# Value products of an attention kernel as two tiles of 64 features, with a new order in its slots

## The chip, the cores and the metric

The kernel runs on one core of a Trainium2 chip. The metric is the device time of one execution, in microseconds (us). Below, PE is the tensor engine's matmuls, PEld its weight loads, DVE the vector engine, ACT the scalar engine, POOL the GpSimd engine, and SP the engine whose queue issues the DMAs; SPq is that queue.

## The reference, cut to what matters

```python
def phi(x):
    proj = np.einsum('bhsd,df->bhsf', x, w_phi)                    # d = 64, f = 128
    proj = proj - np.max(np.abs(proj), axis=-1, keepdims=True)
    return np.concatenate([np.exp(proj), np.exp(-proj)], axis=-1)  # 256 features
q_p, k_p = phi(q), phi(k)                    # batch 4, heads 8, sequence 576
kv = np.einsum('bhsf,bhsd->bhfd', k_p, v)
z = np.sum(k_p, axis=2)
num = np.einsum('bhsf,bhfd->bhsd', q_p, kv)
den = np.einsum('bhsf,bhf->bhs', q_p, z)[..., None] + 1e-06
x = num / den                                # then [2304, 512]
h = (x @ w1) * (x @ w2) @ w3 @ w_out         # first MLP
y = np.maximum(h @ w_in, 0.0) ** 2 @ w_out2  # second MLP
```

The MLP weights arrive as 64-bit floats and are decoded on the chip.

## The kernel before, in words

Attention is worked off in 16 units t = 0 to 15, one for each pair of heads of a batch (`todo`). The sequence of 576 is cut in 512 and a tail of 64; the tails of two units are handled together, in the even unit. A list of words, `SLOT` (L32 to L38), is the order of the work in a slot: for each t the loop at L668 calls the step of every word in turn, and a step adds its instructions at the end of the queue of each engine that it uses. A word works on unit t plus an offset (`steps`, L594): `project_q`, `max_q`, `minus_q`, `values0` on unit t; `turn_k`, `turn_q` on t+1; `out`, `feature_sums`, `denominators`, `reciprocals`, `quotients` on t-1; `store_x` on t-2; the loads on t+2. Words that begin with w (`w0`, `w1`, `w-1`) advance the decoding of one weight tile by a step: a DMA of raw words, an ACT copy, twice two DVE operations (L107/L110 and L114/L117), a POOL addition, an ACT copy, a POOL subtraction. `START` (L28) holds words that run ahead of the first slot. Each engine works its queue strictly in this order.

A slot begins on PE with `project_q` (L371): for both heads and for the tail, three passes each (high by high, high by low, low by high parts), into the tile pq (three PSUM banks, one buffer: the next unit's `project_q` can't write until the `exp_q` steps of this unit have read it). Then `project_k` (pk, L243), `turn_k` and `turn_q` (transposes, L279), `max_rows` (pm, L386), `out` (po, L446, two matmuls of 64 output features side by side), `feature_sums` (pd: L461 with four tiles of 32, then L467 with two tiles of 64), `minus_q` (L405), `values` (pkv, L420 and for the tail L429).

The maximum of a row of q takes a way round: `max_q` on DVE (L378), a transpose on PE (L386), `max_parts` on DVE (L391 to L394), two DMAs from mh into the row tile mrow (L397), and `minus_q`, which adds it to pq with a matmul. Then ACT exponentiates pq twice, `exp_q0` and `exp_q1` (L412). For k, `peak_k` (DVE, L339) and `less_k` (DVE, L349) lead to `exp_k` (ACT, L356), which makes kp, the stationary operand of `values`; part 2 of k (the tails) exists in even slots only.

`values` loads 128 features by 128 positions of kp for each matmul and streams 65 columns of v and ones:

```python
for s in range(2):
    for c in range(C):
        nc.tensor.matmul(
            z["pkv"][:, s, j], z["kp", j][:, c, s, :], z["vs"][:, j, c, :],
            start=j + s + c == 0, stop=False, skip_group_check=True,
        )
```

These are fp32 matmuls, and the profile shows each as two records of weight load and matmul: 32 for a unit's 16 matmuls of `values` and 4 for its tail.

In the last slots the words that occur once (`once`, L639) add the beginning of the first MLP: x is loaded back (`x_load`), split in high and low parts (`x_split0` to `x_split3`), and multiplied (`product_a0`, `product_a1`, `product_b`). From `prefetch` (L553) raw weight words for the MLPs are loaded on the same SP queue as `store_x` (L518), which stores the finished x of two units. The MLPs follow from about 232 us on and are not touched, apart from the place of one store.

Of the kernel before, what the change touches and what calls it, by code (L numbers as in the profile page):

```python
# [9 lines left out]
F32 = mybir.dt.float32  # L10
# [16 lines left out]

START = """  # L28
turn_q/-1 turn_k/-1 high_q/-1 high_k/-1 turn_tails/-1 low_q/-1 low_k/-1 keep_tails/-1 low_tail/-1
""".split()  # L30
SLOT = """
load_kq product_b project_q keep_values project_k0 turn_w3b split_w3b x_load max_q project_k1 w1 w1 w0 turn_k peak_k0  # L32
max_rows x_split0 high_k max_parts w-1 store_x less_k0 out x_split2 exp_k0 feature_sums x_split1 peak_k1 less_k1
keep turn_q low_k turn_tails project_k2 exp_k1 denominators spread high_q peak_k2 less_k2 minus_q keep_tails
values0 gate turn_w3 x_split3 low_q w0 exp_q0 exp_k2 w0 exp_q1 w0 product_a0 values1 keep_rest low_tail reciprocals
split_w3 product_a1 quotients keep_a load_v tail_values
""".split()


# [1 line left out]
def attention_then_mlps(ctx: ExitStack, tc: tile.TileContext, q, k, v, w_phi, w1, w2, w3, wo, wi2, wo2, out):  # L41
# [155 lines left out]
    with ExitStack() as actx:  # L197
# [55 lines left out]
        def load_kq(t):  # L253
            (b, pr), z = todo[t], live[t]
            z["nm"], z["b"], z["pr"] = f"{b}_{pr}", b, pr
            z["before"] = live[t - 1] if t else None
            z["qm"] = load_q(b, pr)
            z["km"] = load_k(b, pr)
            if pr == 0:
                tails[b] = load_tail(q, b, "qtl"), load_tail(k, b, "ktl")  # L260
            z["qt"], z["kt"] = tails[b]
# [98 lines left out]
        def project_q(z):  # L360

            pr = z["pr"]
            z["pq"] = ps.tile([P, 3 * 512], F32, tag="q", bufs=1, name=f"pq_{z['nm']}")
            z["pv"] = z["pq"][:, 0:2 * S]
            tT = (z if pr % 2 == 0 else z["before"])["tT"]
            r = pr % 2
            sides = [(j, j * C * P, z["qT"], C * P) for j in range(2)] + [(r, 2 * C * P, tT, P)]
            for n, (a, b) in enumerate(((0, 0), (0, 1), (1, 0))):
                for j, at, src, width in sides:
                    h = slice(j * D, (j + 1) * D)  # L370
                    nc.tensor.matmul(  # L371
                        z["pq"][:, at:at + width], wss[h, b, :], src[h, a, 0:width], start=n == 0, stop=n == 2
                    )

        def max_q(z):

# [32 lines left out]
        def exp_q(z, s):  # L409
            if s == 0:  # L410
                z["qp"] = att.tile([P, 2, 2 * S], F32, tag="qp", name=f"qp_{z['nm']}")
            nc.scalar.activation(z["qp"][:, s], z["pv"], AF.Exp, scale=1.0 - 2.0 * s)  # L412

        def values(z, j):

            if j == 0:
                z["pkv"] = bank(f"pkv_{z['nm']}")[:, 0:4 * (D + 1)].rearrange("p (s j d) -> p s j d", s=2, j=2)
            for s in range(2):
                for c in range(C):
                    nc.tensor.matmul(  # L420
                        z["pkv"][:, s, j], z["kp", j][:, c, s, :], z["vs"][:, j, c, :],
                        start=j + s + c == 0, stop=False, skip_group_check=True,
                    )

        def tail_values(z):
            pr = z["pr"]
            kpt = z["kp", 2] if pr % 2 == 0 else z["before"]["kp", 2]
            for s in range(2):
                nc.tensor.matmul(  # L429
                    z["pkv"][:, s].rearrange("p j d -> p (j d)"), kpt[:, pr % 2, s, :],  # L430
                    z["vt"][:, pr].rearrange("p j d -> p (j d)"), start=False, stop=True, skip_group_check=True,
                )

        def keep_values(z):

# [15 lines left out]
        def feature_sums(z):  # L451

            z["pd"] = pd = bank(f"pd_{z['nm']}", "o", 2)
            for e in range(2):
                for i in range(4):
                    j, s = divmod(i, 2)
                    for k, (at, of, n) in enumerate(
                        ((0, j * C * P, HALF),) if s == 0 else
                        ((0, j * C * P + HALF, C * P - HALF), (C * P - HALF, 2 * C * P + j * TAIL, TAIL))
                    ):  # L460
                        nc.tensor.matmul(  # L461
                            pd[i * 32:(i + 1) * 32, at:at + n], z["zs"][:, e, j, :], z["qp"][:, e, of:of + n],
                            start=e + k == 0, stop=e == 1, skip_group_check=True,
                        )
            for e in range(2):
                for j in range(2):
                    nc.tensor.matmul(  # L467
                        pd[j * D:(j + 1) * D, HALF:HALF + TAIL], z["kv"][:, e, j, :],
                        z["qp"][:, e, 2 * C * P + j * TAIL:2 * C * P + (j + 1) * TAIL],
                        start=False, stop=e == 1, skip_group_check=True,  # L470
                    )

        def keep(z):
            z["nd"] = att.tile([P, S], F32, tag="nd", name=f"nd_{z['nm']}")
# [4 lines left out]

        def denominators(z):  # L480

            dc = att.tile([P, nb // 2], F32, tag="dc", name=f"dc_{z['nm']}")
            nc.vector.tensor_reduce(
                dc, z["pd"][:, 0:HALF].rearrange("p (n r) -> p n r", r=32), AX.X, ALU.max, apply_transpose=True
            )
# [76 lines left out]
        beside = [decode_splitting(rows(wo, j), f"wo{j}", wos) for j in range(NG)]  # L562
        beside += [decode_splitting(*w12_of(i), w12) for i in range(6)]
        beside += [decoding(*w3_of(i), w3s) for i in range(4)]
        load_kq(0)
# [5 lines left out]
        wst = att.tile([D, F], F32, bufs=1, name="wst")  # L571
        nc.sync.dma_start(wst, w_phi)
# [91 lines left out]
        with tc.manual_schedule(engines=mine):  # L664
# [226 lines left out]
    with tc.manual_schedule(engines=mine):  # L891
# [5 lines left out]
        for s, (grp, at, k) in enumerate(steps):  # L897
# [157 lines left out]
```

## Time and profile before

| what | us |
|---|---|
| median of 3 runs (lowest, highest) | 993.65 (989.38, 996.88) |
| the profiled execution's own time | 995.93 |
| its span from first to last instruction | 994.2 |
| PE busy in the span | 969.9 |
| DVE, ACT, POOL busy | 550.3, 377.8, 239.5 |

The profile is of one execution. Its span is divided by the start of `project_q` into a start of 9.2 us, the slots 0 to 15 up to about 225 us, a transition, and the MLPs. A row of a timeline gives start, length, engine, line, operation, tiles and, in brackets, how long the engine was idle before and what ended that. A row of windows gives the stretch and its length, then the busy time (and count) of PE, PEld, DVE, ACT and POOL, the granted clock of PE as a share of full speed, the share of the DMA engines in use and the GB/s.

### The profile page before, as it was taken

What the parts mean: (1) busy time and instruction counts of PE and PEld (TensorE: products, weight loads), DVE (VectorE), ACT (ScalarE), POOL (GpSimd) and SP (SyncE); (2) the same over time, 40 slices, a digit from 0 to 9 for tenths busy, and PEclk for the clock granted to TensorE, in tenths of its full rate; (3) what the DMA queues carried; (4) which work ended last, traced back from release to release, by engine and by line L of the source; (5) the groups of instructions that cost most, each with busy time, mean ns of one, the idle gap of its engine ahead of it and who ended that gap; (6) DMA issues with size and microseconds to landing.
All of it is one profiled execution on the core that took longest, in us unless ns stands there. A gap on an engine that the chain in (4) does not pass through costs nothing.

```text
span 994.2 us, 13665 instructions
## 1 busy us (share of the span) xinstructions
PE 969.9 (98%) x5304; PEld 796.1 (80%) x5304; DVE 550.3 (55%) x908; ACT 377.8 (38%) x689; POOL 239.5 (24%) x304
## 2 busy tenths in 40 slices
PE   6999999998999999999999999999999999999997
PEld 5788787776888898888888888888888888888896
DVE  5668888776665546566675487873223222322332
ACT  3556666663332233343333243442223212322322
POOL 2345555524222112333332135540000000000000
PEclk8879999999899999999999999999999999999999
DMA  5344545533323223424444432312000100100010
GB/s 146 95 117 133 144 134 144 159 108 104 108 86 127 64 106 127 149 102 152 149 170 154 164 106 91 100 43 84 1 1 32 55 1 0 64 1 1 1 43 22
DMA packets 81105, 89.16 MB, mean 90 GB/s; under 512 B 44624, under 2 KB 65680, under 8 KB 81040
## 3 DMA queue, kind: packets, MB, share of 16 engines
q1 hardware_dynamic: 81040, 88.28, 27.9%
q8 instruction: 42, 0.69, 0.3%
q14 instruction: 23, 0.19, 0.1%
HBM read 69.76 MB, written 18.35 MB: 89 GB/s over the span
## 4 chain that ended last, share of the span: by engine, by line
PE 93%; DMA 3%; DVE 2%; issue 1%; ACT 0%; SPq 0%; DVEq 0%; ACTq 0%
PE op L875 20%; PE ph L176 20%; PE yp L857 10%; PE pb L176 9%; PE pa L176 9%; PE pkv L420 6%; PE pf L814 4%; PE pk L243 3%; PE po L446 2%; PE pq L371 2%; DMA mrow<-mh 1%; PE pd L461 1%; PE pq L405 1%; PE pkv L429 1%; PE pw L170 1%; PE pkt L279 1%
## 5 line engine op out<-in xcount | busy, mean ns | idle before, releaser
L875 PE MATMUL op<-w_w,r 128*128 128x512 f32 x864 | 214.5, 396 | 0.0
L875 PEld LDWEIGHTS op<-w_w,r 128*128 128x128 f32 x864 | 161.5, 188 | 37.4 <-ACT r L1005 0.5
L176 PE MATMUL ph<-y,w_w 128*128 128x512 f32 (+1 forms) x768 | 166.6, 366 | 0.0
L999 DVE SCALAR_TENSOR_TENSOR r<-ph,t 128x512 f32<-128x512 f32 (+1 forms) x80 | 51.1, 638 | 196.0 <-ACT t L997 196.0
L176 PEld LDWEIGHTS ph<-y,w_w 128*128 128x128 f32 x768 | 133.6, 189 | 26.5
L997 ACT ACTIVATE t<-ph 128x512 f32<-128x512 f32 (+1 forms) x80 | 44.4, 555 | 224.2 <-PE ph L176 224.2
L857 PE MATMUL yp<-g,w3o 128*128 128x512 f32 (+1 forms) x480 | 109.4, 378 | 0.0
L857 PEld LDWEIGHTS yp<-g,w3o 128*128 128x128 f32 x480 | 85.4, 192 | 16.4
L176 PE MATMUL pa<-c,w_w12a 128*128 128x512 f32 (+1 forms) x432 | 95.7, 369 | 0.8 <-ACT c L141 0.8
L176 PE MATMUL pb<-c,w_w12b 128*128 128x512 f32 (+1 forms) x432 | 93.9, 367 | 0.0
L122 POOL TENSOR_TENSOR dt_w<-dt_w,dy_w 128x512 f32<-128x512 f32 x48 | 62.7, 1306 | 123.5 <-DVE dy_w L117 122.4
L176 PEld LDWEIGHTS pa<-c,w_w12a 128*128 128x128 f32 x432 | 75.0, 189 | 16.4 <-ACT c L141 1.1
L176 PEld LDWEIGHTS pb<-c,w_w12b 128*128 128x128 f32 x432 | 75.2, 189 | 13.4
L1007 DVE TENSOR_TENSOR r<-r,r 128x512 fp32r<-128x512 f32 (+1 forms) x80 | 51.0, 638 | 41.2 <-ACT r L1005 37.0
L936 DVE TENSOR_TENSOR g<-pb,a 128x512 f32<-128x512 f32 (+1 forms) x39 | 24.8, 636 | 86.6 <-PE pb L176 86.4
L132 POOL TENSOR_TENSOR w_w<-dt_w,w_w 128x512 fp32r<-128x512 f32 x32 | 48.8, 1525 | 89.8 <-ACT w_w L130 89.8
L1005 ACT ACTIVATE r<-r 128x512 fp32r<-128x512 f32 (+1 forms) x80 | 47.2, 590 | 55.5 <-DVE r L999 55.5
L420 PE MATMUL pkv<-vs,kp 128*128 128x65 f32 x512 | 65.0, 289 | 0.0
L420 PEld LDWEIGHTS pkv<-vs,kp 128*128 128x128 f32 x512 | 63.6, 206 | 0.8
L496 POOL COPY rc<-rc 32x9 f32<-32x9 f32 x128 | 35.7, 279 | 90.4 <-DVE rc L488 85.9
L938 ACT ACTIVATE g<-g 128x512 fp32r<-128x512 f32 (+1 forms) x39 | 23.0, 589 | 90.7 <-DVE g L936 90.7
L356 ACT ACTIVATE kp<-kp 128x512 f32<-128x512 f32 (+1 forms) x80 | 46.9, 587 | 17.4 <-DVE kp L349 16.1
(134 smaller groups left out, 1312.2 us busy)
## 6 DMA issues: line engine op xcount, KB each, us to landing
x<-x_hbm SPq DMA_DIRECT2D x16, 512.0 KB
raw_w<-in_moe_w_dram SPq DMA_DIRECT2D x16, 512.0 KB
raw_w<-in_moe_w_in_dram SPq DMA_DIRECT2D x16, 512.0 KB
raw_w<-in_moe_w_out_dram SPq DMA_DIRECT2D x16, 512.0 KB
qm<-in_q_dram SPq DMA_DIRECT2D x32, 128.0 KB
km<-in_k_dram SPq DMA_DIRECT2D x16, 256.0 KB
vs<-in_v_dram SPq DMA_DIRECT2D x32, 128.0 KB
raw_wo<-in_moe_w_out_dram SPq DMA_DIRECT2D x8, 512.0 KB
```

Source lines behind the costliest of these rows:

```text
L122: nc.gpsimd.tensor_tensor(out=w, in0=t.bitcast(F32), in1=e.bitcast(F32), op=ALU.add)
L132: nc.gpsimd.tensor_tensor(out=dst[:, 1], in0=w[0], in1=dst[:, 0].bitcast(F32), op=ALU.subtract)
L176: nc.tensor.matmul(ps[:, 0:n], a, c, start=kk + i == 0, stop=kk == KD - 1 and i == 2)
L356: nc.scalar.activation(z["kp", j][:, :, s, :], z["kp", j][:, :, 1, :], AF.Exp, scale=1.0 - 2.0 * s)
L420: nc.tensor.matmul(z["pkv"][:, s, j], z["kp", j][:, c, s, :], z["vs"][:, j, c, :], start=j + s + c == 0, stop=False, skip_group_check=True,)
L814: nc.tensor.matmul(pf, a, c, start=g + j + n == 0, stop=g == 1 and j == 3 and n == 2)
L857: nc.tensor.matmul(blk.yp[i][:, 0:blk.n], a, d, start=c % HG + s == 0, stop=c % HG == HG - 1 and s == 2)
L875: nc.tensor.matmul(ops[i], a, d, start=j + s == 0, stop=j == NR - 1 and s == 2)
L997: nc.scalar.activation(t[:, 0:n], ph[:, 0:n], AF.Relu)
L999: nc.vector.scalar_tensor_tensor(out=r32[:, 0:n], in0=ph[:, 0:n], scalar=0.0, in1=t[:, 0:n], op0=ALU.max, op1=ALU.mult)
L1005: nc.scalar.activation(r[:, 0, 0:n], r32[:, 0:n], AF.Copy)
L1007: nc.vector.tensor_tensor(out=r[:, 1, 0:n], in0=r32[:, 0:n], in1=r[:, 0, 0:n].bitcast(F32), op=ALU.subtract)
```

## The change

`values` and `tail_values` issue each matmul as two, one for each half of the features, which go to two column tiles of the PE array beside each other. `project_q` does all three passes of the heads before those of the tail. `feature_sums` puts L467 ahead of L461. The addition of 1e-6 moves from DVE to POOL, into the eight copies of `spread`, and the reciprocal moves behind these, into `reciprocals`. The load of w_phi is issued behind the loads of the first q. `SLOT` gets another order: `less_k0` ahead of `max_parts`; `exp_k0` ahead of `out`; `high_q`, then `exp_k2`, ahead of `keep_tails` and `exp_q0` on ACT; the splits of x behind `exp_k0`; `product_a0` ahead of `minus_q`. The first slot gets its own order through `START`. The last `store_x` is issued after the second step of the first MLP.

```diff
 START = """
 turn_q/-1 turn_k/-1 high_q/-1 high_k/-1 turn_tails/-1 low_q/-1 low_k/-1 keep_tails/-1 low_tail/-1
+project_q/0 project_k0/0 project_k1/0 max_q/0 peak_k0/0 less_k0/0 exp_k0/0 max_rows/0 max_parts/0 load_kq/0 w-1/0
+turn_q/0 turn_k/0 high_q/0 peak_k1/0 less_k1/0 low_q/0 project_k2/0 exp_k1/0 high_k/0 low_k/0 peak_k2/0 less_k2/0 values0/0 exp_k2/0
 """.split()
 SLOT = """
 load_kq product_b project_q keep_values project_k0 turn_w3b split_w3b x_load max_q project_k1 w1 w1 w0 turn_k peak_k0
-max_rows x_split0 high_k max_parts w-1 store_x less_k0 out x_split2 exp_k0 feature_sums x_split1 peak_k1 less_k1
-keep turn_q low_k turn_tails project_k2 exp_k1 denominators spread high_q peak_k2 less_k2 minus_q keep_tails
-values0 gate turn_w3 x_split3 low_q w0 exp_q0 exp_k2 w0 exp_q1 w0 product_a0 values1 keep_rest low_tail reciprocals
-split_w3 product_a1 quotients keep_a load_v tail_values
+max_rows high_k less_k0 max_parts w-1 store_x exp_k0 out x_split0 x_split1 x_split2 feature_sums peak_k1 less_k1
+keep turn_q low_k turn_tails project_k2 product_a0 exp_k1 denominators spread peak_k2 less_k2 high_q minus_q exp_k2
+keep_tails exp_q0 values0 gate turn_w3 x_split3 low_q w0 w0 exp_q1 w0 values1 keep_rest low_tail reciprocals split_w3
+product_a1 quotients keep_a load_v tail_values
 """.split()
...
             z["qm"] = load_q(b, pr)
+            if t == 0:
+                nc.sync.dma_start(wst, w_phi)
             z["km"] = load_k(b, pr)
...
-            sides = [(j, j * C * P, z["qT"], C * P) for j in range(2)] + [(r, 2 * C * P, tT, P)]
-            for n, (a, b) in enumerate(((0, 0), (0, 1), (1, 0))):
-                for j, at, src, width in sides:
-                    h = slice(j * D, (j + 1) * D)
-                    nc.tensor.matmul(
+            for sides in ([(j, j * C * P, z["qT"], C * P) for j in range(2)], [(r, 2 * C * P, tT, P)]):
+                for n, (a, b) in enumerate(((0, 0), (0, 1), (1, 0))):
+                    for j, at, src, width in sides:
+                        h = slice(j * D, (j + 1) * D)
+                        nc.tensor.matmul(
...
+        halves_f = [slice(0, F // 2), slice(F // 2, F)]
+
         def values(z, j):
...
             for s in range(2):
                 for c in range(C):
-                    nc.tensor.matmul(
-                        z["pkv"][:, s, j], z["kp", j][:, c, s, :], z["vs"][:, j, c, :],
-                        start=j + s + c == 0, stop=False, skip_group_check=True,
-                    )
+                    for h in halves_f:
+                        nc.tensor.matmul(
+                            z["pkv"][h, s, j], z["kp", j][:, c, s, h], z["vs"][:, j, c, :],
+                            start=j + s + c == 0, stop=False, skip_group_check=True,
+                        )
...
-            dc = att.tile([P, nb // 2], F32, tag="dc", name=f"dc_{z['nm']}")
+            z["dc"] = att.tile([P, nb // 2], F32, tag="dc", name=f"dc_{z['nm']}")
...
-            nc.vector.tensor_scalar(out=dc, in0=dc, scalar1=1e-6, scalar2=None, op0=ALU.add)
-            z["rc"] = att.tile([P, nb // 2], F32, tag="rc", name=f"rc_{z['nm']}")
-            nc.vector.reciprocal(z["rc"], dc)
...
-                    nc.gpsimd.tensor_copy(
-                        z["rc2"][i * 32:(i + 1) * 32, s, :], z["rc"][at * 32:(at + 1) * 32, :]
+                    nc.gpsimd.tensor_scalar(
+                        out=z["rc2"][i * 32:(i + 1) * 32, s, :], in0=z["dc"][at * 32:(at + 1) * 32, :],
+                        scalar1=1e-6, scalar2=None, op0=ALU.add,
                     )
 
         def reciprocals(z):
+            nc.vector.reciprocal(z["rc2"], z["rc2"])
...
-                    if f"{name}/{t}" not in START:
+                    if f"{name}/{t}" not in START and not (name == "store_x" and t > len(todo)):
                         step(name, t)
...
                 fold.product()
+            if s == 1:
+                store_x(live[-1])
```

`tail_values` is cut in two as `values` is, and in `feature_sums` the loop of L467 stands ahead of that of L461 with the start flags moved.

## Rows read from the trace of the kernel before

**Rows 1.** The page, busy time of the engines over the span.
```profile
PE 969.9 (98%) x5304; PEld 796.1 (80%) x5304; DVE 550.3 (55%) x908; ACT 377.8 (38%) x689; POOL 239.5 (24%) x304
```

**Rows 2.** Windows, one a slot: slots 0 to 3, 8, 9, and 15.
```profile
9.20:27.50 18.30, 15.85 (x73) 14.34 (x73) 9.53 (x18) 6.69 (x11) 1.27 (x1) 0.76 0.55 146
27.50:41.75 14.25, 14.25 (x112) 11.63 (x111) 9.87 (x19) 8.03 (x15) 4.44 (x10) 0.83 0.34 93
41.75:57.70 15.95, 14.78 (x113) 12.13 (x112) 10.34 (x21) 8.57 (x16) 8.26 (x15) 0.85 0.41 105
57.70:72.40 14.70, 14.70 (x114) 11.98 (x113) 9.95 (x19) 8.03 (x15) 4.61 (x10) 0.82 0.45 132
...
121.50:133.80 12.30, 12.30 (x114) 9.88 (x114) 10.38 (x21) 8.58 (x16) 6.13 (x13) 1.00 0.41 110
133.80:146.00 12.20, 12.20 (x114) 9.83 (x113) 9.84 (x19) 8.12 (x15) 6.67 (x13) 1.00 0.53 152
...
208.70:233.00 24.30, 22.02 (x178) 16.39 (x177) 12.54 (x24) 11.82 (x22) 6.42 (x14) 1.00 0.33 110
```

**Rows 3.** Timeline of PE in slot 8 and the first row of slot 9.
```profile
127.87 0.45 PE L467 MATMUL pd<-qp,kv 128*64 128x64 f32 x8
128.25 0.66 PE L279 MATMUL pqt<-ident,qm 128*128 128x128 f32 x4
128.67 0.60 PE L243 MATMUL pk<-wbd,tT 128*128 128x256 f32 x3
129.10 0.69 PE L405 MATMUL pq<-mrow,minus 128*128 128x512 f32 x3
129.63 3.73 PE L420 MATMUL pkv<-vs,kp 128*128 128x65 f32 x32
133.20 0.67 PE L429 MATMUL pkv<-vt,kp 128*128 128x130 f32 x4
133.79 0.73 PE L371 MATMUL pq<-qT,wss 64*128 64x512 f32 x3
```

**Rows 4.** Timeline of ACT in slots 8 and 9.
```profile
129.83 1.13 ACT L412 ACTIVATE qp<-pq 128x1152 f32<-128x1152 f32 x1
130.86 0.86 ACT L356 ACTIVATE kp<-kp 128x256 f32<-128x256 f32 x2
131.62 1.11 ACT L412 ACTIVATE qp<-pq 128x1152 f32<-128x1152 f32 x1
...
142.17 2.15 ACT L412 ACTIVATE qp<-pq 128x1152 f32<-128x1152 f32 x2
```

**Rows 5.** Timeline of DVE in slots 8 and 9.
```profile
125.59 0.67 DVE L349 TENSOR_TENSOR kp<-pk,kmax 128x512 f32<-128x512 f32 x1
...
129.30 0.42 DVE L339 TENSOR_REDUCE kmax<-pk 128x2 f32<-128x256 f32 x1
129.76 0.42 DVE L349 TENSOR_TENSOR kp<-pk,kmax 128x256 f32<-128x256 f32 x1
...
135.08 1.38 DVE L378 TRANSPOSE_TENSOR_REDUCE m<-pq 128x36 f32<-128x1152 f32 x1 [1.36 <-PE pq L371]
```

**Rows 6.** The chain that ended last, in order of time: three waits for a DMA.
```profile
48.59 1.91 DMA mrow<-mh
...
213.80 3.32 DMA mrow<-mh
...
242.12 4.87 DMA raw_w12b<-in_moe_w_dram
```

**Rows 7.** Waits of the SP queue, 215 to 256 us: total, times, longest.
```profile
SPq L521 <- POOL xm L511: 16.5, 1, 16.5
```

**Rows 8.** Windows of two stretches in which the granted clock was half.
```profile
18.70:32.35 13.65, 13.65 (x61) 12.70 (x62) 5.39 (x9) 6.16 (x12) 2.54 (x2) 0.50 0.34 93
...
52.83:63.07 10.24, 10.24 (x48) 9.48 (x47) 3.17 (x4) 3.21 (x8) 4.04 (x4) 0.50 0.36 90
```

**Rows 9.** Timeline of PE in slot 0, its value products.
```profile
19.52 7.03 PE L420 MATMUL pkv<-vs,kp 128*128 128x65 f32 x32
```

More of the change, by code (lines that the diff above doesn't have):

```diff
@@ L366, in project_q @@
             r = pr % 2
-            sides = [(j, j * C * P, z["qT"], C * P) for j in range(2)] + [(r, 2 * C * P, tT, P)]
-            for n, (a, b) in enumerate(((0, 0), (0, 1), (1, 0))):
-                for j, at, src, width in sides:
-                    h = slice(j * D, (j + 1) * D)
-                    nc.tensor.matmul(
-                        z["pq"][:, at:at + width], wss[h, b, :], src[h, a, 0:width], start=n == 0, stop=n == 2
-                    )
+            for sides in ([(j, j * C * P, z["qT"], C * P) for j in range(2)], [(r, 2 * C * P, tT, P)]):
[3 more added lines that the diff above has]
+                        nc.tensor.matmul(
+                            z["pq"][:, at:at + width], wss[h, b, :], src[h, a, 0:width], start=n == 0, stop=n == 2
+                        )
         def max_q(z):
@@ L419, in values @@
                 for c in range(C):
-                    nc.tensor.matmul(
-                        z["pkv"][:, s, j], z["kp", j][:, c, s, :], z["vs"][:, j, c, :],
-                        start=j + s + c == 0, stop=False, skip_group_check=True,
-                    )
+                    for h in halves_f:
+                        nc.tensor.matmul(
+                            z["pkv"][h, s, j], z["kp", j][:, c, s, h], z["vs"][:, j, c, :],
+                            start=j + s + c == 0, stop=False, skip_group_check=True,
+                        )
         def tail_values(z):
@@ L428, in tail_values @@
             for s in range(2):
[L429 to L432, printed above, removed]
+                for h in halves_f:
+                    nc.tensor.matmul(
+                        z["pkv"][h, s].rearrange("p j d -> p (j d)"), kpt[:, pr % 2, s, h],
+                        z["vt"][:, pr].rearrange("p j d -> p (j d)"), start=False, stop=True, skip_group_check=True,
+                    )
         def keep_values(z):
@@ L454, in feature_sums @@
             for e in range(2):
+                for j in range(2):
+                    nc.tensor.matmul(
+                        pd[j * D:(j + 1) * D, HALF:HALF + TAIL], z["kv"][:, e, j, :],
+                        z["qp"][:, e, 2 * C * P + j * TAIL:2 * C * P + (j + 1) * TAIL],
+                        start=e == 0, stop=e == 1, skip_group_check=True,
+                    )
+            for e in range(2):
                 for i in range(4):
                     j, s = divmod(i, 2)
-                    for k, (at, of, n) in enumerate(
+                    for at, of, n in (
                         ((0, j * C * P, HALF),) if s == 0 else
@@ L462, in feature_sums @@
                             pd[i * 32:(i + 1) * 32, at:at + n], z["zs"][:, e, j, :], z["qp"][:, e, of:of + n],
-                            start=e + k == 0, stop=e == 1, skip_group_check=True,
+                            start=False, stop=e == 1, skip_group_check=True,
                         )
[L465 to L471, printed above, removed]
         def keep(z):
@@ L480, in denominators @@
         def denominators(z):
-            dc = att.tile([P, nb // 2], F32, tag="dc", name=f"dc_{z['nm']}")
+            z["dc"] = att.tile([P, nb // 2], F32, tag="dc", name=f"dc_{z['nm']}")
             nc.vector.tensor_reduce(
-                dc, z["pd"][:, 0:HALF].rearrange("p (n r) -> p n r", r=32), AX.X, ALU.max, apply_transpose=True
+                z["dc"], z["pd"][:, 0:HALF].rearrange("p (n r) -> p n r", r=32), AX.X, ALU.max, apply_transpose=True
             )
-            nc.vector.tensor_scalar(out=dc, in0=dc, scalar1=1e-6, scalar2=None, op0=ALU.add)
-            z["rc"] = att.tile([P, nb // 2], F32, tag="rc", name=f"rc_{z['nm']}")
-            nc.vector.reciprocal(z["rc"], dc)
         def spread(z):
@@ L564, in attention_then_mlps @@
         beside += [decoding(*w3_of(i), w3s) for i in range(4)]
+        wst = att.tile([D, F], F32, bufs=1, name="wst")
         load_kq(0)
@@ L570, in attention_then_mlps @@
         nc.vector.memset(mrow.bitcast(F32), 0.0)
-        wst = att.tile([D, F], F32, bufs=1, name="wst")
-        nc.sync.dma_start(wst, w_phi)
         wss = att.tile([P, 2, F], F32R, bufs=1, name="wss")
```

## The prediction

> **What bounds the kernel now.** I read the busy times first, then the windows slot by slot, then the timelines of PE, ACT and DVE in two neighbouring slots, last the chain of waits. PE is busy for 98% of the span [rows 1], so time goes only where PE gets less to do or waits less. The windows show where the change can act [rows 2]: only the slots of attention, up to about 233 us; the MLPs keep their work. [...] DVE is busy for 10.38 of 12.30 us in slot 8 and 9.84 of 12.20 in slot 9, ACT for 8.6 and 8.1: a slot that gets two microseconds shorter leaves them little room. That is the heart of this case: PE's saving is easy to see, what is late next decides how much of it is kept.
>
> **The value products.** In slot 8 they run from 129.63 to 133.20, 32 records in 3.57 us, 111.6 ns each [rows 3], though each streams only 65 columns. The nearest row to the new form is L467: a 64-feature tile with 64 columns, two tiles side by side; 8 of them take 128.25 - 127.87 = 0.38 us, and this holds one change of the array's tile form. With p for one matmul and c for a change, 8p + c = 0.38. At p = 28 ns (a quarter of 111.6: half the features, two at once) c is 0.16; at c = 0, p is 47.5. I take p = 31 ns, near the lower end because the two tiles of L467 are as independent as the new ones, and c = 0.13. The 64 new records take 64 x 31 ns = 1.98 us, and PE saves 1.59 a slot (1.78 at 28 ns, 0.53 at 47.5). Entering the new form costs one c; putting L467 directly behind `out`, which has the same form, saves one c. The two cancel. The tail goes from 4 records in 133.79 - 133.20 = 0.59 us to 8 with two times the columns of L467, 8 x 62 ns = 0.50: counted as nothing (a gain of 0.09, a loss of 0.17 at 47.5).
>
> [...]
>
> **project_q.** The same nine matmuls in another order; one of 512 columns takes about 0.73/3 = 0.24 us [rows 3], and no more than one such can be won or lost. I take nothing: what the order does is to let the heads start while the tail's low part is still being made on DVE.
>
> **What is late next, in an even slot.** pq has one buffer, so `project_q` of the next unit waits for `exp_q1`. Now ACT does `exp_q0`, `exp_k2`, `exp_q1`, up to 132.73, a microsecond ahead of PE at 133.79 [rows 3, 4]. In the new order `exp_k2` comes first. The tail's pk is done at 128.67 + 0.60 = 129.27, earlier by c = 129.14. DVE then has no addition and reciprocal ahead of it: kmax and the subtraction take 0.46 + 0.42 [rows 5], to 130.02; `exp_k2` 0.86, to 130.88; the two `exp_q` together 2.15 [rows 4], to 133.03. PE would be ready at 133.79 - 1.59 = 132.20. So PE waits 0.8 us, and an even slot saves 133.79 - 133.03 = 0.76 instead of 1.59.
>
> **In an odd slot** there is no `exp_k2`. The two `exp_q` of slot 9 begin at 142.17 and end at 144.32; PE, done at 146.00 - 1.59 = 144.41, is not held. Here `less_k0` (0.67) ahead of `max_parts` [rows 5] sends mrow off by up to 0.67 us later; minus_q is not waited for in these slots now, so that costs between 0 and 0.67, and I take 0.1. DVE waited 1.36 us for `max_q` in slot 9 [rows 5]; that slack is used up, the addition's time goes to POOL, which is busy for half of a slot [rows 2], and DVE is level with PE. An odd slot saves 1.5.
>
> Slots 4 to 14 are six even and five odd: 6 x 0.76 + 5 x 1.5 = **12.1 us**.
>
> **Slots 1 to 3** take 14.25 + 15.95 + 14.70 = 44.9 us, and the clock costs 0.17 x 14.25 + 0.15 x 15.95 + 0.18 x 14.70 = 7.4 of them [rows 2]. The order saves 1.5 + 0.76 + 1.5 = 3.8. The clock fell twice to half, each time after PE had stood or had run value products: for 13.65 us from 18.70, where nearly all of slot 0's value products lie, and for 10.24 us from 52.83, some 2 us after a wait for mrow [rows 6, 8]. With half as much time in value products I expect about half of that cost to go, 3.7 (bounds 0 and 7.4). Together **7.5**.
>
> **Start and slot 0.** The value products take 7.03 us there, at half clock [rows 8, 9]; 64 x 62 ns = 4.0 saves 3.0. PE is idle for 18.30 - 15.85 = 2.45 us in the slot [rows 2]; the new first order puts `max_parts` ahead of the next unit's transposes and `values0` ahead of `minus_q`, so the way of mrow is covered by work that was there anyway. Against this stands the wait for `exp_q1` as in every even slot, here without work from a slot before to cover it: 0.86 + 2.15 [rows 4] after a late `less_k2`; I put it at 1.5. Net **4.0** (bounds 1 and 6.5). The load of w_phi comes earlier, but PE's queue waits for the tails just ahead of `project_q`: nothing.
>
> **Slot 15** has 24.30 - 22.02 = 2.3 us of idle, of which the wait for mrow at 213.80 is most [rows 2, 6]. The later splits of x let `max_parts` and k go ahead, and `product_a0` fills the wait; its matmuls were there already. The value products save 1.6, the idle time 2.3, and three splits on ACT ahead of `exp_k1` give about 1.2 back: **2.7** (bounds 1 and 4).
>
> **The last store.** SP stood 16.5 us for the xm that it stores [rows 7], with two loads of words queued behind. With the store gone the first can go as soon as its buffer is free. But the chain hangs on the second, raw_w12b, issued at 242.12 [rows 6], and that waits for a buffer which DVE frees then, not for the store. It only shares the DMA with one tile less of three: at most a third of 4.87; I take **0.7**.
>
> Sum: 12.1 + 7.5 + 4.0 + 2.7 + 0.7 = 27.0. The profiled execution took 995.93, 2.3 above the median of 993.65; its 995.93 - 27.0 = 968.9 stands for 966.6, in round numbers **966 us**. About 1% (10 us) is what a measurement of this kernel can tell from no change.
>
> **The rivals.**
> A. PE sets every slot: the wait for `exp_q1` does not come. For it: ACT is busy for only 8.6 of 12.3 us; against it: the chain above has no gap. Then six even slots save 0.8 more (4.8), slot 0 1.5, slot 2 0.8, and the clock keeps up, 3.7: 955. Chance 0.2.
> B. The clock falls more often. PE gets a pause of 0.8 us in every even slot. Against it: slot 15's pause of 2 us at 213.80 was followed by no fall before 247 us, in windows at full clock. Two more stretches as that of 52.83 cost 2 x 10.24/2 = 10.2: 976. Chance 0.13.
> C. The other side: PE can't be fed so fast. L467 shows 31 to 47 ns for eight in a row, not for 64; the trace's longest run of such pairs of load and matmul is at 111.6 ns. Above 111.6/2 = 55.8 ns a half costs more than it saves. At 111.6 the value products take 7.14 us, 3.57 more in 16 slots: +57, less some 7 that the rest still saves: 1044; at 70 ns 64 x 70 = 4.48, +0.9 in 16 slots, +15, or about 1002. Chance 0.04.
> [...]
> D. The change does not do what it says: the two loads of 64 features take as long together as one of 128, the value products stay at 3.57 us, and only start, idle time and store are won, about 6: 988. Chance 0.05.
>
> **How the numbers follow.** The forecast has 0.58; its own range is 959 to 974 (the bounds of the clock's 3.7 and of slot 0). The range reaches into A and B: 953 to 980. Faster by over 1%: 0.58 + 0.2 + 0.12 of B = 0.90; within 1%: D and the edge of B, 0.06; slower by over 1%: C, 0.04.
>
> **What would show it right or wrong.** Right: pkv's 64 records of a slot in about 2.0 us; in even slots PE idle for 0.8 us ahead of L371, released by ACT's L412, and none in odd ones; slots of 11.5 and 10.7 us in turn; no SP wait for xm ahead of raw_w. Wrong: pkv at 3 us or more; idle time ahead of L405 (mrow) or DVE without any idle time in all slots, which would put the bound there; a granted clock of half in slots 4 to 14.

## The result and the profile after

The changed kernel took 963.07 us (median of 4 runs, 961.57 to 964.43), the kernel before 995.26 beside it (4 runs, 989.38 to 997.28). The forecast was 966 us. The ratio is 0.9686, with a 95% interval of 0.9639 to 0.9732: by it 31 us less, where 27 had been forecast. The profiled execution took 963.54 us, with a span of 961.8 against 994.2.

The page of the changed kernel, busy times and the chain that ended last by engine:

```profile
PE 935.5 (97%) x5880; PEld 760.2 (79%) x5880; DVE 547.4 (57%) x892; ACT 382.5 (40%) x689; POOL 249.5 (26%) x304
...
PE 88%; DVE 4%; ACT 3%; DMA 2%; issue 1%; SPq 0%; DVEq 0%; ACTq 0%
```

PE has 576 records more than in [rows 1] (36 more a slot in 16 slots) and is busy for 969.9 - 935.5 = 34.4 us less, more than the 32.4 by which the span is shorter. PE is still what sets the end.

Windows of the changed kernel, one a slot: 0, 1, 2, 3, 8, 9 and 15, then the transition from `product_b` to the first MLP's second group (columns as in [rows 2]):

```profile
8.40:22.66 14.26, 10.20 (x109) 8.15 (x110) 9.26 (x18) 7.38 (x13) 0.00 (x0) 0.99 0.78 203
22.66:36.07 13.41, 13.41 (x149) 10.60 (x149) 8.52 (x16) 8.09 (x15) 5.27 (x10) 0.75 0.30 81
36.07:47.54 11.47, 10.78 (x149) 8.28 (x149) 10.82 (x22) 8.75 (x17) 7.09 (x13) 1.00 0.57 144
47.54:58.12 10.58, 10.58 (x149) 8.21 (x149) 8.96 (x17) 8.52 (x16) 6.90 (x12) 1.00 0.63 178
...
102.14:113.57 11.43, 10.73 (x149) 8.25 (x150) 10.73 (x22) 8.75 (x17) 6.99 (x14) 1.00 0.52 143
113.57:124.82 11.25, 10.66 (x149) 8.19 (x149) 9.65 (x19) 8.52 (x16) 7.50 (x13) 1.00 0.55 148
...
181.27:195.36 14.09, 13.70 (x153) 9.83 (x154) 9.66 (x18) 9.41 (x19) 4.69 (x11) 1.00 0.42 130
195.36:222.28 26.92, 23.43 (x125) 17.86 (x126) 21.90 (x35) 9.21 (x19) 13.30 (x17) 0.94 0.39 123
```

The reader is to see three things. In the even slot 8, PE has 0.70 us without work (11.43 - 10.73), where [rows 2] have none. Only one of the slots shown is still at 0.75 of the clock, where [rows 2] have four at 0.76 to 0.85. And slot 15 has 0.39 us of idle time left.

I cut both profiled executions at the starts of `project_q` and of the matmuls that follow, and took the differences:

| stage | before | after | less | forecast |
|---|---|---|---|---|
| start and slot 0 | 27.45 | 22.66 | 4.8 | 4.0 |
| slots 1 to 3 | 44.9 | 35.4 | 9.5 | 7.5 |
| slots 4 to 14 | 136.3 | 123.2 | 13.1 | 12.1 |
| slot 15 | 16.75 | 14.09 | 2.7 | 2.7 |
| `product_b` to second group of the first MLP | 29.15 | 26.75 | 2.4 | 0.7 |
| the rest of the MLPs | 739.6 | 739.65 | 0 | 0 |

A slot of `project_q` to `project_q` was 12.26 us (even) and 12.11 (odd) before, where nothing disturbed it, and is 11.50 and 10.50 now.

Timeline of PE in the changed kernel: the end of slot 0, then of slots 8 and 9:

```profile
18.24 1.15 PE L427 MATMUL pkv<-vs,kp 128*64 128x65 f32 x32
...
22.66 1.65 PE L375 MATMUL pq<-qT,wss 64*128 64x512 f32 x6 [2.17 <-ACT qp L416]
...
110.33 2.09 PE L427 MATMUL pkv<-vs,kp 128*64 128x65 f32 x64
112.25 0.61 PE L437 MATMUL pkv<-vt,kp 128*64 128x130 f32 x8
113.57 0.96 PE L375 MATMUL pq<-qT,wss 64*128 64x512 f32 x6 [0.70 <-ACT qp L416]
...
121.60 0.76 PE L409 MATMUL pq<-mrow,minus 128*128 128x512 f32 x3 [0.59 <-DMA mrow<-mh]
```

and of ACT at the end of slot 8:

```profile
110.61 0.87 ACT L360 ACTIVATE kp<-kp 128x256 f32<-128x256 f32 x2 [0.57 <-DVE kp L353]
111.38 2.13 ACT L416 ACTIVATE qp<-pq 128x1152 f32<-128x1152 f32 x2
```

The 64 records of the value products last 112.25 - 110.33 = 1.92 us, 30.0 ns each, against 3.57 us in [rows 3]. Behind them PE stands for 0.70 us for `exp_q1`, which ends 111.38 + 2.13 = 113.51 and follows `exp_k2` without a gap. In the odd slot 9 PE stands for mrow, 0.59 us, which it did not in slot 9 before. Of slots 4 to 14 PE waits for `exp_q1` in 4, 8 and 12, and for mrow in 6, 9, 10, 13 and 14. That wait does not lengthen the even slots 6 and 14 (11.50 us), since ACT's three exponentials follow each other there as they do in slot 8; slot 10, with 1.28 us of waiting for mrow, takes 12.04. PE's wait in slot 6:

```profile
88.21 0.76 PE L409 MATMUL pq<-mrow,minus 128*128 128x512 f32 x3 [0.56 <-DMA mrow<-mh]
```

Windows of the stretches at half clock in the changed kernel, up to the MLPs; there are two:

```profile
22.53:29.36 6.83, 6.70 (x28) 5.59 (x30) 3.70 (x7) 2.48 (x7) 2.55 (x2) 0.51 0.36 83
217.00:220.40 3.40, 3.29 (x9) 2.52 (x10) 3.33 (x7) 1.20 (x3) 1.28 (x1) 0.50 0.49 149
```

Against [rows 8], with 13.65 and 10.24 us, attention itself has one, of 6.83 us, which begins at the end of the 2.17 us that PE stood ahead of slot 1. The waits of slots 4 to 14, of up to 1.28 us, were followed by none.

Timelines of SP's queue and of ACT in the changed kernel, at the last store:

```profile
206.93 0.38 SPq L100 DMA_DIRECT2D raw_w12a<-in_moe_w_dram  x1
211.56 0.38 SPq L100 DMA_DIRECT2D raw_w12b<-in_moe_w_dram  x1
215.26 0.66 ACT L107 ACTIVATE dy_w12b<-raw_w12b 128x512 f32<-128x512 f32 x1 [4.02 <-DMA raw_w12b<-in_moe_w_dram]
219.38 0.42 SPq L528 DMA_DIRECT2D x_hbm<-xm  x1
```

The second load of raw words, raw_w12b, takes 215.26 - 211.56 = 3.70 us to its reader, where [rows 6] show 4.87, and the store follows behind it. The first load, raw_w12a, goes 4.6 us ahead of it and has its reader at 210.56, before the second is issued.

### The profile page after: what moved, and what is told of

Read it like the earlier page. It is cut to its first block, busy times and chain, and to the rows that moved or that the text cites. A ratio compares the mean times of both kernels' runs of the same rounds, so it can differ in the third digit from the quotient of the medians.

```text
span 961.8 us, 14797 instructions
## 1 busy us (share of the span) xinstructions
PE 935.5 (97%) x5880; PEld 760.2 (79%) x5880; DVE 547.4 (57%) x892; ACT 382.5 (40%) x689; POOL 249.5 (26%) x304
## 4 chain that ended last, share of the span: by engine, by line
PE 88%; DVE 4%; ACT 3%; DMA 2%; issue 1%; SPq 0%; DVEq 0%; ACTq 0%
PE ph L178 21%; PE op L881 21%; PE yp L863 10%; PE pb L178 10%; PE pa L178 9%; PE pf L820 4%; PE po L454 3%; PE pk L245 3%; PE pq L375 2%; PE pkv L427 2%; ACT qp L416 1%; PE pd L476 1%; DMA mrow<-mh 1%; DVE kmax L343 1%; ACT kp L360 1%
## 5 line engine op out<-in xcount | busy, mean ns | idle before, releaser
L501 POOL TENSOR_SCALAR rc<-dc 32x9 f32<-32x9 f32 x128 | 45.3, 354 | 63.6 <-DVE dc L491 56.7
L934 ACT COPY a<-pa 128x512 f32<-128x512 f32 (+1 forms) x39 | 21.2, 543 | 83.7 <-PE pa L178 83.7
L116 DVE TENSOR_SCALAR dy_w<-dt_w 128x512 int32<-128x512 int32 x48 | 51.0, 1063 | 0.7
```

The source lines that it names most:

```text
L116: nc.vector.tensor_scalar(out=e, in0=t, scalar1=-(1 << 23), scalar2=None, op0=ALU.bitwise_and)
L501: nc.gpsimd.tensor_scalar(out=z["rc2"][i * 32:(i + 1) * 32, s, :], in0=z["dc"][at * 32:(at + 1) * 32, :], scalar1=1e-6, scalar2=None, op0= ...
```

## The experiments

My theory going in was that the two tiles bring nearly all, the orders little, and that what ends last in an even slot is `exp_q1`. The rivals were that the orders carry a good part, that half clock is made by whole value products, and that PE could be fed no faster. The moves inside `SLOT`, the addition on POOL and the earlier load of w_phi were not run one by one. The runs were made in groups, each with the kernel before beside it, so across groups the ratios say more than differences between medians.

**Orders alone.** The new orders with whole value products:

```diff
-        halves_f = [slice(0, F // 2), slice(F // 2, F)]
+        halves_f = [slice(0, F)]
```

> The changed kernel with the value products as whole matmuls of 128 features again, all orders kept. Theory (the tiles shorten PE by 1.5 us a slot, and of that an even slot keeps only what the wait for exp_q1 leaves): even slots go from 11.4 to about 12.2 us, odd ones from 10.6 to about 12.0, the waits of L375 for exp_q1 vanish, the total rises by 17 to 24, to 980 to 987. Rival 1 (PE's saving is kept whole in every slot): 1.55 in 16 slots, 25 or more, 988 and up. Rival 2 (the orders do most of it): at most 5 more, 968.

990.12 us (10 runs), ratio 0.9973 (0.995 to 0.9996). The undisturbed slots are 12.12 and 12.11 us, close to what the theory gave, but the total is higher than its range. In the profiled execution the 72.3 us up to slot 4 have become 61.0, so 11.3 are won there; slot 13 gives 19.29 - 13.41 = 5.9 of them back, and slot 14, which the same half-clock stretch reaches, 14.09 - 12.27 = 1.8 more. Windows of slot 13:

```profile
182.02:195.67 13.65, 12.87 (x56) 12.06 (x57) 4.03 (x8) 3.87 (x7) 5.49 (x7) 0.50 0.20 65
195.67:200.00 4.33, 4.33 (x51) 2.77 (x50) 3.83 (x8) 2.86 (x5) 0.00 (x0) 1.00 0.03 6
```

and its timeline of PE:

```profile
182.80 1.30 PE L409 MATMUL pq<-mrow,minus 128*128 128x512 f32 x3 [2.78 <-DMA mrow<-mh]
183.90 7.03 PE L427 MATMUL pkv<-vs,kp 128*128 128x65 f32 x32
190.72 1.18 PE L437 MATMUL pkv<-vt,kp 128*128 128x130 f32 x4
191.83 1.65 PE L375 MATMUL pq<-qT,wss 64*128 64x512 f32 x6
193.94 2.46 PE L245 MATMUL pk<-wbd,kT 128*128 128x256 f32 x12
```

PE stood for 2.78 us for mrow, the clock fell, and then 8 us of whole value products, with no gap in them, ran at half clock; it was back only at 195.67, after `project_q` and most of `project_k`. So the total is as high as it is mostly by this stretch. Slots 4 and 5, with waits for mrow of 0.6 and 0.4 us, add 1.2 us.

**The tiles alone.** The kernel before, with its matmuls of `values` and `tail_values` cut in two:

```diff
+                    for h in (slice(0, F // 2), slice(F // 2, F)):
                         nc.tensor.matmul(
-                            z["pkv"][:, s, j], z["kp", j][:, c, s, :], z["vs"][:, j, c, :],
+                            z["pkv"][h, s, j], z["kp", j][:, c, s, h], z["vs"][:, j, c, :],
```

> The kernel before with the two tiles of 64 features alone. Theory: odd slots about 10.8 us, even ones 11.4 to 11.6, because PE now waits for exp_q1 there; with some of the slow clock gone, the total is 970 to 978. Rival 1 (nothing is late next): even and odd slots both 10.7, 966 or less. Rival 2 (the tiles need the new order): no more than 10 won, 985 or more.

966.19 us (4 runs), ratio 0.9732 (0.9698 to 0.9767): 27 of the 31 us. Undisturbed slots are 11.75 and 10.80 us. The total is some us under the theory's range, for there is less half clock than it counted: one stretch in attention, where the kernel before has two. The stretch at half clock and what follows it, by windows:

```profile
18.08:24.91 6.83, 6.09 (x78) 5.08 (x76) 4.29 (x8) 5.82 (x10) 0.57 (x1) 0.50 0.32 100
24.91:30.00 5.09, 5.09 (x36) 3.36 (x34) 3.55 (x7) 2.62 (x6) 1.99 (x2) 1.00 0.53 129
```

and by the timeline of PE:

```profile
20.40 3.74 PE L421 MATMUL pkv<-vs,kp 128*64 128x65 f32 x64
23.93 1.08 PE L431 MATMUL pkv<-vt,kp 128*64 128x130 f32 x8
24.94 0.73 PE L371 MATMUL pq<-qT,wss 64*128 64x512 f32 x3
```

The clock falls at nearly the same place as before [rows 8], ahead of the same work, and is back after 6.83 us instead of 13.65, as `project_q` begins.

Slot 4 begins at 72.3 us in the kernel before, at 61.0 with the orders alone, at 58.1 with the tiles alone, and at 58.0 with both (56.8 in a second profile). The gains alone, 11.3 and 14.2, do not add up, because a good part of each is the same half clock taken away.

**The last store put back** to its slot:

```diff
-                    if f"{name}/{t}" not in START and not (name == "store_x" and t > len(todo)):
+                    if f"{name}/{t}" not in START:
...
-            if s == 1:
-                store_x(live[-1])
```

> The changed kernel with the last store of x at its old place ahead of the words. Theory (the second load of words, raw_w12b, shares the DMA with the store and the load that it held up): raw_w12b lands 4.9 us after its issue again instead of 3.7, PE's wait ahead of pw L172 is about 5 us instead of 3.4, the total rises by 1.2 to 3. Rival (the shorter DVE queue brought the words earlier, the store does nothing): less than 0.5 either way, the wait stays at 3.4.

963.97 us (4 runs), ratio 0.9709 (0.9677 to 0.9741). The times do not tell it from the changed kernel; the rows do. Timelines of SP's queue and of ACT with the store put back:

```profile
209.62 0.33 SPq L528 DMA_DIRECT2D x_hbm<-xm  x1
210.12 0.38 SPq L100 DMA_DIRECT2D raw_w12a<-in_moe_w_dram  x1
211.41 0.38 SPq L100 DMA_DIRECT2D raw_w12b<-in_moe_w_dram  x1
...
216.30 0.66 ACT L107 ACTIVATE dy_w12b<-raw_w12b 128x512 f32<-128x512 f32 x1 [1.15 <-DMA raw_w12b<-in_moe_w_dram]
```

The load of raw_w12b is issued at the same time as in the changed kernel (211.41 and 211.56) and lands 1.2 us later, 4.89 us after its issue instead of 3.70. It did not wait for the store. The load of raw_w12a, which the store had held up (210.12, where the changed kernel has 206.93), was on its way beside it: ACT waited for it until 214.48, 3.07 us behind the issue of raw_w12b. The store was issued 1.79 us ahead of raw_w12b; the run does not tell the parts of the two from each other. PE's wait for the first MLP's words is 4.6 us here and 3.4 in the changed kernel.

**The first slot's order taken out:** the two lines added to `START` are removed.

```diff
-project_q/0 project_k0/0 project_k1/0 max_q/0 peak_k0/0 less_k0/0 exp_k0/0 max_rows/0 max_parts/0 load_kq/0 w-1/0
-turn_q/0 turn_k/0 high_q/0 peak_k1/0 less_k1/0 low_q/0 project_k2/0 exp_k1/0 high_k/0 low_k/0 peak_k2/0 less_k2/0 values0/0 exp_k2/0
```

> The changed kernel with START as before, so the first slot has the order of all others. Theory: slot 0 loses what values0 ahead of minus_q and max_parts ahead of the transposes covered, 1.5 to 4 us; slots 4 to 15 stay as they are; 964.5 to 967. Rival 1 (the new start holds the clock up): the granted clock falls for longer in slots 0 to 3, and 5 to 10 us are lost, up to 973. Rival 2 (the order of the start does nothing, the earlier w_phi does it): no change.

963.51 us (4 runs), ratio 0.9714 (0.9674 to 0.9754): no different from the changed kernel. Slot 0 takes 15.69 us instead of 14.0, but a half-clock stretch of 6.8 us then lies inside it, and slot 1 is free of it (the granted clock is 0.78 in slot 0 and 1.00 in slot 1; in the changed kernel it is 0.99 and 0.75): slot 4 begins at 56.8 us, as in a second profile of the changed kernel. In these profiles the first slot's order only moves the place where the clock is lost. What the earlier load of w_phi does was not tried by itself.

**`exp_k2` behind `exp_q1`**, so that pq comes free earlier:

```diff
-keep turn_q low_k turn_tails project_k2 product_a0 exp_k1 denominators spread peak_k2 less_k2 high_q minus_q exp_k2
-keep_tails exp_q0 values0 gate turn_w3 x_split3 low_q w0 w0 exp_q1 w0 values1 keep_rest low_tail reciprocals split_w3
+keep turn_q low_k turn_tails project_k2 product_a0 exp_k1 denominators spread peak_k2 less_k2 high_q minus_q
+keep_tails exp_q0 values0 gate turn_w3 x_split3 low_q w0 w0 exp_q1 exp_k2 w0 values1 keep_rest low_tail reciprocals split_w3
```

> The changed kernel with exp_k2 behind both exp_q on ACT (it was ahead of them). Theory (an even slot is as long as the chain pk of the tails, kmax, less_k2, exp_k2, exp_q0, exp_q1): the wait of L375 for exp_q1 vanishes and a wait of the tail's value products (L437) for exp_k2 of about 1.2 us takes its place, an even slot goes from 11.5 to about 11.9, seven of them cost 2 to 4: 965 to 967. Rival (ACT's busy time as such or mrow sets the even slots): the even slots stay at 11.5 and no wait of L437 appears; a PE bound would make them 10.7.

967.19 us (4 runs), ratio 0.9746 (0.9708 to 0.9784). PE's waits in this kernel (total, times, longest):

```profile
PE pq L409 <- DMA mrow<-mh: 5.9, 7, 1.2
...
PE pkv L437 <- ACT kp L360: 3.2, 6, 0.5
...
PE pq L375 <- ACT qp L416: 2.2, 1, 2.2
```

and in the changed kernel:

```profile
PE pq L375 <- ACT qp L416: 4.5, 5, 2.2
PE pq L409 <- DMA mrow<-mh: 3.9, 6, 1.3
PE pw L172 <- ACT a L934: 3.4, 1, 3.4
```

The wait of `project_q` is gone but for slot 0's 2.2 us, and the tail's value products wait for `exp_k2` in its place, in up to 0.5 us where I had put more. Even slots are 11.74 where undisturbed, not shorter: ACT's three exponentials are one chain, and whoever is last is waited for. Four of the six even slots from 4 to 14 take 12.55 to 12.87, because a wait for mrow of 0.8 to 1.2 us comes on top, and slots 4 to 14 together take 5 us more than in the changed kernel.

**Whole value products in the first four slots only:**

```diff
-                    for h in halves_f:
+                    for h in (halves_f if live.index(z) >= 4 else [slice(0, F)]):
...
-                for h in halves_f:
+                for h in (halves_f if live.index(z) >= 4 else [slice(0, F)]):
```

> The changed kernel with whole value products in units 0 to 3, halves from unit 4 on. [...] Rival (the fall comes from the idle time before, the form of the value products has no part in it): 1.2 to 1.5 a slot alone, 4 to 6, 967 to 969, with no more half clock than in the changed kernel.

968.39 us (4 runs), ratio 0.9771 (0.9734 to 0.9808). Slots 0 to 3 take 14.01, 13.49, 13.56 and 12.15 us. My theory here was that whole value products make the clock fall in these slots, which would have given 974 to 977 us. It is refuted, and the total is the rival's: the only half-clock stretch in attention of the profiled execution is 3.4 us from 22.6, behind the value products and after a wait. The mean granted clocks of the four runs, 0.991 to 0.996, are those of the changed kernel (0.991 to 0.997 in ten runs). Its window and, below it, the timeline of PE:

```profile
22.60:26.00 3.40, 3.40 (x16) 3.00 (x17) 1.54 (x2) 1.46 (x4) 2.33 (x2) 0.50 0.75 178
```

```profile
18.70 1.95 PE L427 MATMUL pkv<-vs,kp 128*128 128x65 f32 x16
20.48 0.66 PE L437 MATMUL pkv<-vt,kp 128*128 128x130 f32 x4
22.49 1.56 PE L375 MATMUL pq<-qT,wss 64*128 64x512 f32 x6 [1.35 <-ACT qp L416]
```

Sixteen whole records in 20.48 - 18.70 = 1.78 us are 111 ns each, as in slot 8 of the kernel before, where the granted clock was 1.00 [rows 2, 3]: full clock. What is lost against the changed kernel (5 us by the medians, 8 by the ratios) lies in these slots: slot 4 begins at 61.7 us, 3.6 and 4.9 later than in the two profiles of the changed kernel, and slots 4 to 14 take the same 123.0. Slot 2 is 13.56 - 11.54 = 2.0 us longer and slot 3 12.15 - 10.51 = 1.6, at full clock in both kernels; slot 0, which hangs on waits, is no longer.

**Four tiles of 32 features** instead of two of 64, to see whether feeding PE is a bound:

```diff
-        halves_f = [slice(0, F // 2), slice(F // 2, F)]
+        halves_f = [slice(i * F // 4, (i + 1) * F // 4) for i in range(4)]
```

> The changed kernel with the value products in four tiles of 32 features, 128 records a unit. Theory (halves are already bound by the streaming of their 65 columns in two passes, which four tiles do not shorten; what is left is whether PE is fed): at best 2.0 us again, if loads and matmuls can follow each other twice as fast; if the 31 ns of a half were the rate at which PE can be fed, 128 x 31 = 4.0 us, and each slot 2 us longer, 990 or more. Rival (a slot is still bound by the loads of weights, 64 columns a load): shorter, 1.2 to 1.5 us.

981.64 us (one run), 18 above the changed kernel. Timeline of PE in slot 7:

```profile
103.77 2.05 PE L427 MATMUL pkv<-vs,kp 128*32 128x65 f32 x128
105.63 0.63 PE L437 MATMUL pkv<-vt,kp 128*32 128x130 f32 x16
...
108.93 0.73 PE L375 MATMUL pq<-qT,wss 64*128 64x512 f32 x3 [2.02 <-issue]
```

128 records take 105.63 - 103.77 = 1.86 us, 14.5 ns each, and as long as the 64 of the changed kernel. So at 30 ns the changed kernel's halves were not held by the issue of instructions: twice as many were taken in the same time. But behind them PE stands for 2.02 us in the middle of `project_q` for something that the profile calls issue (twice in `project_q` and twice in the value products themselves, 7.2 us in all), and the clock falls to half five times instead of two (over the whole run it is 0.988, against 0.994). What the issue waits for was not tried. The trace has a hint: each of the four stalls begins 0.3 to 0.9 us behind the start of one of the 16 KB transfers on the DMA queue that the page calls instruction, and ends 1.3 to 1.5 us behind its end. The page counts 55 of them in this kernel and 46 in the changed one. So PE may have stood for its own instructions; the trace shows the coincidence, not the cause.

**A version that beats both,** by about 3 us. `project_k2` goes to the front, so that DVE and ACT come to `exp_k2` sooner:

```diff
-turn_q/0 turn_k/0 high_q/0 peak_k1/0 less_k1/0 low_q/0 project_k2/0 exp_k1/0 high_k/0 low_k/0 peak_k2/0 less_k2/0 values0/0 exp_k2/0
+turn_q/0 turn_k/0 high_q/0 peak_k1/0 less_k1/0 low_q/0 project_k2/0 exp_k1/0 peak_k2/0 less_k2/0 exp_k2/0 high_k/0 low_k/0 values0/0
...
-max_rows high_k less_k0 max_parts w-1 store_x exp_k0 out x_split0 x_split1 x_split2 feature_sums peak_k1 less_k1
-keep turn_q low_k turn_tails project_k2 product_a0 exp_k1 denominators spread peak_k2 less_k2 high_q minus_q exp_k2
+max_rows high_k less_k0 max_parts w-1 store_x exp_k0 out x_split0 x_split1 x_split2 feature_sums project_k2 peak_k1 less_k1
+keep turn_q low_k turn_tails product_a0 exp_k1 denominators spread peak_k2 less_k2 high_q minus_q exp_k2
```

> The changed kernel with project_k2 ahead of turn_q (so that less_k2 and exp_k2 come sooner), and in the first slot's order exp_k2 ahead of high_k. Theory (even slots hang on that chain): each even slot 0.3 to 0.4 us shorter, the wait of L375 for exp_q1 smaller by as much, slot 0 shorter by about 1; 959 to 961. Rival (mrow or DVE takes its place at once): even slots stay within 0.1 of 11.5, the wait moves to L409; 962 to 963.

961.37 us (4 runs), ratio 0.9697 (0.9663 to 0.973). Undisturbed even slots are 11.12 us, slot 0 is 12.87. PE's waits in this kernel:

```profile
PE pq L409 <- DMA mrow<-mh: 6.4, 8, 1.2
...
PE pq L375 <- ACT qp L416: 2.4, 3, 1.6
```

The wait for `exp_q1` falls from 4.5 to 2.4 us, and that for mrow grows from 3.9 to 6.4: what is won is given back to the next in line. Slots 4 to 14 show it: they take 122.9 us here and 123.2 in the changed kernel, so the rival holds for them. What is gained lies ahead of them: slot 4 begins at 55.0 us instead of 58.1, since the wait for `exp_q1` ahead of slot 1 is 1.65 us instead of 2.17 and no half-clock stretch follows it. To see whether the rest is real I ran it again beside the changed kernel, with a second profile of the two other kernels.

> The kernel with project_k2 ahead of turn_q and exp_k2 ahead of high_k in the first slot, beside the changed one. Theory: even slots 11.1 instead of 11.5, seven times 0.4, and slot 0 shorter by 1: 2 to 4 us below the changed kernel. Rival (waits for mrow give it back): within 1 us of it.

> The changed kernel again, beside the next one, and a second profile of its clock. Theory: 962 to 964; one early stretch at half clock of some 3 to 7 us, or none, where it stands differing from execution to execution. Rival (the stretch at 22.5 us belongs to this kernel's order): the same stretch again within 1 us.

961.61 us (6 runs, ratio 0.9657, 0.9624 to 0.9689) beside 964.99 for the changed kernel (6 runs, 0.9691, 0.9655 to 0.9727): about 3 us better in the median. The intervals of the two ratios overlap; the two sets of six runs by themselves differ by 3.1 us in the mean, with a standard error of 0.9. Slot 4 begins at 55.4 us in the second profile of this kernel and at 56.8 in that of the changed one, and slots 4 to 14 are again not shorter (124.6, with one half-clock stretch of 3.4 us in them, and 123.0). So the theory named the wrong place: the gain comes from the start and slots 0 to 3, not from the even slots.

> All orders with whole value products again, for a second profile. Theory (with whole value products the clock falls somewhere in attention in every execution, after a wait for mrow): again one stretch or more at half clock between 20 and 200 us, 10 us or longer in all. Rival (the fall at 182 us was that one execution's): no such stretch, and a time 5 to 7 us below 990.

> The kernel before again, for a second profile of its clock. Theory: again two stretches at half clock in slots 0 to 3, 20 to 24 us in all, since the waits and the value products ahead of them are the same. Rival: their place and length change from execution to execution by more than 7 us.

The orders alone (992.9 us, one run) again had a long half-clock stretch in slot 13, 10.2 us from 186.4, and a short one of 3.4 us from 22.6. The kernel before (997.57 us, one run) had its two again, 13.7 us from 19.6 and 10.2 from 53.8. So the long stretches came in both profiles of these two kernels. The changed kernel's second profile had 3.4 us from 23.9, and 6.8 from 215.1 in the transition.

## Why the prediction was right

The step that carried the forecast held. **The value products** are a matter of two tiles beside each other: 31 ns was taken for a half, 30.0 was measured. The experiment with the tiles alone gives 27 us, the one with the orders alone 3. The change of tile form was taken as c = 0.13 us, by the choice of p; where the changed order has one change less, from `out` to the transposes, slot 9 takes 120.14 - 116.89 = 3.25 us instead of 140.52 - 137.13 = 3.39, which is 0.14 less and agrees.

**An even slot** saves 12.26 - 11.50 = 0.76 us, the forecast's own number, and for its reason: 0.70 us ahead of `project_q` in slot 8, released by `exp_q1` (forecast 0.8), and the run with `exp_k2` last shows that this wait is that chain of ACT. From the end of the tail's pk to the end of `exp_q1` it was forecast at 3.89 us and took 113.51 - 109.65 = 3.86, with the pk's row at 109.05 for 0.60 us. Rival A, in which the wait does not come, is out by this row. **An odd slot** saves 12.11 - 10.50 = 1.61 where 1.5 was taken; the later mrow, priced at 0.1, costs nothing in an undisturbed slot and 0.6 in such as slot 9. PE's waits in slots 4 to 14 of the changed kernel:

```profile
PE pq L409 <- DMA mrow<-mh: 3.5, 5, 1.3
PE pq L375 <- ACT qp L416: 2.0, 3, 0.7
```

The same stretch before had 1.5 us in 3 waits for mrow and none for `exp_q1`. So the sign "none in odd slots" failed in slots 9 and 13, the waits for mrow in the even slots 6, 10 and 14 were not foreseen at all, and a small part of the gain goes into them. With the tiles alone, in the old order, the same slots have 2.1 us in 3 such waits, so not all of them come from the later mrow. The margin that the prediction gave PE in odd slots was none: it took PE's end from the window's edge, 146.00, where `project_q` stands at 145.91, so that PE and `exp_q1` were level at 144.32. Slots 4 to 14 came to 13.1 instead of 12.1.

**Slots 1 to 3** saved 9.5 (10.9 by the second profile) instead of 7.5. The working had two terms. The clock costs 0.25 x 13.41 = 3.4 us there now, of 7.4 before, so 4.0 went by it (half, 3.7, was taken); the rest, 5.5, went by work and waits, where 3.8 was taken. The mis-sized term is the second: undisturbed slots alone save 1.61 + 0.76 + 1.61 = 4.0, and slot 2 had 15.95 - 14.78 = 1.17 us of idle time [rows 2] which I did not count and which went as well; the 0.3 that remain are within what such shares of a clock can tell. In the reason for the clock I was half wrong: less time in value products fits a stretch that is shorter once it has begun (the last section has the rows), but the run with whole products in the first four slots shows that they do not begin one.

**Start and slot 0:** 4.8 for 4.0, which is luck, for the terms failed one by one. The value products were priced at half clock (4.0 us); they ran at full clock, 1.15 us for 32 in two lots, since the clock fell only behind them. In exchange the wait for `exp_q1` was 2.17 us, not 1.5, and half clock in slot 1 followed it. "PE is idle for 2.45 us, the new first order covers it" failed altogether: PE is idle for 14.26 - 10.20 = 4.06 us in slot 0, and taking the order out cost nothing by the end of slot 3.

**Slot 15** came to the 2.7 that were worked out, but not by the three terms: PE's idle time fell from 2.28 to 0.39 us, 1.9 where 2.3 was taken, PE's busy time fell by 0.8 where 1.6 was taken, and the 1.2 us that the splits were to give back did not show. **The last store** came out as its run shows, with the size too small: the load lands 1.2 us sooner (3.70 us after its issue, 4.89 with the store put back), where 0.7 was taken. The prediction left one transfer of three out; in the changed kernel raw_w12a had gone 4.6 us ahead as well, so that two were gone. The whole transition shortened by 2.4 us, in a second profile by 1.0; between these two the half-clock stretch in it differs, 3.4 us in the first and 6.8 in the second, as in the kernel before.

Rival B, more falls of the clock, is out: fewer came, one in attention instead of two. Rival C, PE not fed fast enough, is out by the 30.0 ns a half, held over 64 records, and by the 14.5 ns of the quarters. Rival D is out by the 1.92 us.

## What to carry to other kernels

Here a record that streams 65 columns took 111.6 ns against a stationary tile of 128 columns, and two records against 64 columns each, side by side, took 60.0 ns together. Where a matmul streams few columns against a full tile, two column tiles are worth trying, and a row of the same kernel with that form (L467) bounded their price beforehand. When an engine that fills every slot gets shorter work, look for the chain that was a microsecond ahead of it, and count what it takes back; here half of the gain in each even slot. And the gains by the clock did not add up: two edits that each take away the same half-clock stretch are paid once (11.3 and 14.2 us by the start of slot 4 alone, 14.3 together). A faster version deserves a look at where it is faster: the last one here was built for the even slots and won in the start.

## What the runs showed of the hardware that was not expected

How long the clock stayed at half went with the form of the value products that ran in the stretch. Six stretches had whole value products in them, and they lasted 13.65 us (kernel before, from 18.70 and, in the second profile, 19.6; orders alone, from 182.02) or 10.24 us (kernel before, from 52.83 and 53.8; second profile of the orders alone, from 186.4), and PE's records show no gap behind the wait (in [rows 8] PE is busy for all of the 13.65 and of the 10.24 us). Every other stretch in attention and the transition, in all profiles, lasted 6.8 or 3.4 us. That holds with halves in it (6.8 with the tiles alone, from 18.08, and with the first slot's order taken out, from 16.9; 3.4 in slot 13 of the last version) and with no value products in it at all (6.8 in the changed kernel, from 22.5, and 3.4 in its second profile, from 23.9). So halves can't be told from none. All of these stretches began in a wait of PE or at most 2.2 us behind one, but a wait like that was not always followed by one. The granted clock over whole runs goes the same way: 0.986 to 0.993 in ten runs of the orders alone, 0.991 to 0.997 in ten of the changed kernel, and these two kernels differ in the form of the value products alone. That whole value products prolong a stretch once it has begun fits all of these runs, but the form was not varied alone within one stretch, and the reason inside the chip stays open.

A second buffer for pq, which would take the wait for `exp_q1` away altogether, was not tried.
